# Batch 1's keys and queries through the DMA crossbar, in a kernel that joins chunked attention and a feed-forward layer

## The chip, the cores and the metric

The kernel runs on one core of one Trainium2 chip. The metric is the device time of that core in microseconds (us), from several executions. Those of the kernel before lay within 0.4% of their median. Each run has a mean granted TensorE clock (1.0 is full speed). A run counts as slow when it is over 1.5% above the fastest run of its kernel, and as fast otherwise, so that a "fast" run can have a clock below 1.0.

## The reference, cut to what matters

There are 4 batches of 8 heads, 768 tokens and 64 elements a head. Each chunk of 32 queries sees 16 keys to its left, 8 to its right, and 8 memory keys. The attention's output is normalised, and a feed-forward layer (512 to 2048 to 512) is added to it.

```python
for c in range(nc):                                  # nc = 768 / 32 chunks
    q_c = q[:, :, c_start:c_end]
    k_full = concat([mem_k, k[:, :, l_start:r_end]]) # up to 56 + 8 keys
    v_full = concat([mem_v, v[:, :, l_start:r_end]])
    a = softmax(scale * q_c @ k_full.T)
    out[:, :, c_start:c_end] = a @ v_full
# ... [cut: heads side by side give x, 768 x 512 a batch]
xn = (x - mu) / sqrt(var + 1e-06) * g_ln
return x + relu(xn @ w_ch1) @ w_ch2
```

The inputs are small (0.1 times normal numbers), so the softmax is nearly flat.

## The kernel before

The work is cut into 8 units of three tiles of 128 tokens; two units make a batch. Unit u runs its feed-forward matmuls (16 steps of "up", 12 of "down") and carries between its steps the attention of unit u+1 and the preparation of later batches. The function `at(step, ...)` puts a piece of work behind a step; each engine then executes its pieces strictly in that order. TensorE is the engine that is to be kept full.

Keys and queries have to stand with the 64 elements on the partitions before they can be multiplied. Batches 0 and 1 are loaded by rows and turned by TensorE; VectorE and ScalarE copy the result out of PSUM:

```python
    def turn_kq(pv, src, j, n):

        for r in range(8):
            for par in range(2):
                nc.tensor.matmul(
                    out=pv[64 * par : 64 * par + 64, n * r : n * r + n],
                    lhsT=src[0:n, 2 * j + par, r, :],
                    rhs=identity[0:n, 0:n],
                    is_transpose=True, start=True, stop=True,
                    tile_position=(0, 64 * par),
                )
# ...
    def kq_block(b, j, g0, g1, kind):

        pk, pq = slot("att"), None
        if kind == "att":
            pq = slot("att")
            pq = [pq[:, i, :] for i in range(2)]
        else:
            pq = [slot("mm")[:, :] for i in range(2)]
        for i in range(2):
            turn_kq(as16(pk[:, i, :]), k16[b % 2], j + i, 96)
        for i in range(2):
            turn_kq(as16(pq[i]), q16[b % 2], j + i, 96)
# ... [cut: keep_k on VectorE into KT, keep_q on ScalarE into QZ]
```

Batches 2 and 3 are loaded token by partition by GpSimd, turned by a DMA transpose (the "crossbar") issued from the sync queue, and finished by GpSimd, which copies neighbouring keys (`k_around`) and spreads the queries (`spread_q`):

```python
    def load_tokens(b, which, t):
        dst, src = ((kraw[0], k), (qraw[0], q))[which]
        nc.gpsimd.dma_start(
            out=free(dst, 512 * t, [[64, H], [1, 64]]),
            in_=dram(src, b * H * HS + 128 * t * D, [[D, 128], [HS, H], [1, 64]]),
        )

    def cross_k(b, half, t0, t1):
        nc.sync.dma_start_transpose(
            out=free(KT[b % 2], (24 * half + 4 * t0) * KR + 16, [[KR, 4 * (t1 - t0)], [1, 64]]),
            in_=kraw[0][64 * half : 64 * half + 64, 512 * t0 : 512 * t1],
        )

    def cross_q(half, t0, t1):
        nc.sync.dma_start_transpose(
            out=free(QT, (24 * half + 4 * t0) * 64, [[64, 4 * (t1 - t0)], [1, 64]]),
            in_=qraw[0][64 * half : 64 * half + 64, 512 * t0 : 512 * t1],
        )
# ...
    def spread_q(b, half, t0, t1):

        for par in range(2):
            rows = slice(64 * par, 64 * par + 64)
            nc.gpsimd.tensor_copy(
                out=QZ[b % 2][rows, 6 * half + t0 : 6 * half + t1, :, par, :],
                in_=QT[rows, (24 * half + 4 * t0) * 64 : (24 * half + 4 * t1) * 64].rearrange(
                    "p (t j x) -> p t j x", j=4, x=64),
            )
```

Batch 1's values come in 12 group loads, batches 2 and 3's in 8 head loads followed by copies of the edges (`v_around`) on the sync queue, where the outputs (in `down`) and from unit 3 on the transposes of x (`turn_x` with "dma") go too:

```python
    def v_around(b):

        vt = V[b % 2]
        nc.sync.dma_start(out=vt[0:16, 1:NG, :, :], in_=vt[64:80, 0 : NG - 1, :, :])
        nc.sync.dma_start(out=vt[80:88, 0 : NG - 1, :, :], in_=vt[16:24, 1:NG, :, :])
# ...
            nc.sync.dma_start(out=out[t // 6, 128 * (t % 6) : 128 * (t % 6) + 128, :], in_=o)
```

The plan of units 0 to 3, where the change lies:

```python
        if u == 0:
            at(1, clear_q, 1, 0)
            at(5, clear_q, 1, 1)
            at(14, clear_k, 1)
            at(16, clear_v, 1)
            for j in (0, 2):
                at(10 + j, kq_block, 0, j, 6, NG, "att")
                at(11 + j, keep_rest)
            for h in (0, 4):
                for which in range(2):
                    at(12, load_kq, 1, which, 0, 96, h, h + 4)
            for g in range(6):
                at(16, load_v_group, 1, g)
            attend(((16, 19, 19, 22), (17, 21, 21, 24), (19, 23, 23, 26)), "att")
            at(26, mem_cols, 1)
            at(26, v_mem, 1)
        elif u == 1:
            for j in (0, 2):
                at(5 + 3 * j, kq_block, 1, j, 0, NG, "att")
                at(7 + 3 * j, keep_rest)
            for g in range(6, NG):
                at(0, load_v_group, 1, g)
            for t in range(6):
                for which in range(2):
                    at(14, load_tokens, 2, which, t)
            attend(((16, 19, 19, 22), (17, 19, 20, 23), (21, 23, 23, 26)), "att")
        elif following:
            if u in (2, 4):
                attend(((2, 7, 7, 7), (4, 7, 8, 8), (9, 13, 13, 13)))
            else:
                attend(((9, 14, 14, 14), (11, 14, 15, 15), (16, 20, 20, 20)))
            if u == 2:
                cross((0, 0, 1, 1), 2, 0, 4, 3)
                at(8, mem_cols, 2)
                at(8, k_around, 2, 0, 4)
                for h in range(H):
                    at(8, load_v_head, 2, h)
                spread(9, 2, 0, 3)
                cross((14, 14, 15, 15), 2, 4, 6, 6)
            elif u == 3:
                at(1, v_mem, 2)
                at(1, v_around, 2)
                at(4, k_around, 2, 4, 6)
                spread(5, 2, 3, 6)
# ...
        for step in range(16 + 4 * n):
            if step < 16:
                up(u, n, step)
            else:
                i, part = divmod(step - 16, 4)
# ...
            for fn, args in plan.get(step, ()):
                fn(*args)
```

The softmax here doesn't subtract the row's maximum and nothing guards it: scores larger than these inputs give would overflow.

## Time and profile before

| | kernel before |
|---|---|
| median of the first 3 runs | 220.41 us (220.31 to 220.75) |
| median of the 4 runs beside the changed kernel | 220.52 us |
| span of the profiled run | 218.5 us |
| TensorE busy, granted clock | 97%, full |
| waits of TensorE over 0.25 us after unit 0 has begun | none |
| length of units 0 to 6 (first up matmul to the next unit's) | 27.80, 27.28, 23.38, 23.33, 23.35, 23.33, 23.33 us |

In the page, a digit of section 2 is one fortieth of the span, in tenths; the chain (section 4) shares out the span among the engines that held up the end. Units 0 and 1 are longer because their TensorE also turns keys, queries and x.

A transfer "lands" when its semaphore has been raised in full. The landing times of single transfers in this text are read from those updates in the trace; the views print only their medians.

Two timelines of the kernel before matter later. In timelines, columns are start, duration, engine, line, operation, tiles, count; what is in square brackets is the idle time before it and what ended it. First the DMA issues of GpSimd:

```profile
52.80 5.34 POOL L116 DMA_DIRECT2D V<-in_v_dram  x6
58.10 0.96 POOL L241 DMA_DIRECT2D kraw<-in_k_dram  x1
```

and those of the sync queue:

```profile
79.35 2.74 SPq L247 DMA_TRANSPOSE KT<-kraw  x2
82.26 2.61 SPq L253 DMA_TRANSPOSE kraw<-qraw  x2
86.48 6.42 SPq L345 DMA_TRANSPOSE xT<-xn  x3
...
103.51 0.60 SPq L130 DMA_DIRECT2D V<-V  x1
```

Batch 2's token loads start at 58.10. They have all landed by 72.2, so its first key transposes (79.35) find the DMA engines almost idle: issue takes 1.34 and 1.28 us, and the later one lands at 84.25, 3.4 us after its issue began. The edges of batch 2's values (103.51) are the last of that batch's work on the queue.

### The profile page before, as it was taken

The numbers are of one execution on the slowest core, as the hardware profiler recorded it, in microseconds if no ns is written. First come the engines' busy times: TensorE is split into PE (matmuls) and PEld (weight loads), VectorE is DVE, ScalarE is ACT, GpSimd is POOL, SyncE is SP. The second block draws the span as 40 slices with busy tenths as digits, with TensorE's granted clock in tenths as the row PEclk, the third lists the DMA queues.
The fourth block names the chain that finished last, engine by engine and source line by source line (L and its number), as shares of the span: only waits on it lengthen the run. The fifth ranks groups of instructions, "written<-read, shape, count | busy, mean of one in ns | idle before, by whom it ended". The sixth has DMA issues, their size and how long they took to land.

```text
span 218.5 us, 4954 instructions
## 1 busy us (share of the span) xinstructions
PE 212.8 (97%) x1975; PEld 129.2 (59%) x1975; DVE 118.7 (54%) x269; ACT 98.6 (45%) x196; POOL 105.0 (48%) x177
## 2 busy tenths in 40 slices
PE   7998999999999999999999999999999999999994
PEld 2554677556775577545764577446754676457553
DVE  6948566576764836823366339515386337534222
ACT  4464747635884766600555077202751165403200
POOL 7984435957995226986002999626174000300000
PEclk9999999999999999999999999999999999999999
DMA  4999999999999329995605799996743200330012
GB/s 74 181 146 206 208 202 170 192 204 193 178 145 150 105 91 128 163 139 178 87 2 99 106 176 156 162 183 96 174 122 99 96 0 11 88 103 21 0 48 96
DMA packets 93089, 27.20 MB, mean 124 GB/s; under 512 B 83673, under 2 KB 89561, under 8 KB 93018
## 3 DMA queue, kind: packets, MB, share of 16 engines
q0 software_dynamic: 67504, 14.23, 73.9%
q1 hardware_dynamic: 25562, 12.66, 24.7%
q8 instruction: 15, 0.25, 0.5%
q14 instruction: 8, 0.07, 0.1%
HBM read 28.48 MB, written 6.29 MB: 159 GB/s over the span
## 4 chain that ended last, share of the span: by engine, by line
PE 90%; DVE 3%; DMA 3%; ACT 1%; issue 1%; POOL 1%; DVEq 0%; POOLq 0%
PE mm L374 38%; PE mm L391 37%; PE att L288 5%; PE att L308 3%; DMA kraw<-in_k_dram 3%; PE att L178 2%; PE mm L409 2%; DVE xs L319 1%; ACT QZ L203 1%; DVE xn L328 1%; PE att L351 1%; PE mm L178 1%; PE att L365 1%; DVE QZ L203 1%; PE mm L365 0%
## 5 line engine op out<-in xcount | busy, mean ns | idle before, releaser
L374 PE MATMUL mm<-xT,w1c 128*128 128x384 f16 x512 | 88.5, 327 | 0.0
L391 PE MATMUL mm<-w2c,rT 128*128 128x512 f16 x368 | 84.2, 379 | 0.0
L374 PEld LDWEIGHTS <-w1c 128*128 128x128 f16 x512 | 56.8, 114 | 24.3 <-issue 0.3
L380 ACT ACTIVATE rT<-mm 128x384 f16<-128x384 f32 x64 | 31.2, 489 | 68.4 <-PE mm L374 46.8
L391 PEld LDWEIGHTS <-rT 128*128 128x128 f16 x368 | 34.8, 98 | 37.8
L382 DVE TENSOR_SCALAR rT<-mm 128x384 f16<-128x384 f32 x64 | 35.1, 554 | 35.9 <-PE mm L374 35.8
L398 DVE SCALAR_TENSOR_TENSOR osb<-mm,rstd,xs 128x512 f32<-128x512 f32 x23 | 17.3, 751 | 42.3 <-PE mm L391 29.9
L295 ACT ACTIVATE AT<-att,band 96x512 f16<-96x512 f32 x48 | 30.1, 678 | 10.9 <-PE att L288 10.6
L337 POOL TENSOR_SCALAR veps<-squares 128x1 f32<-128x1 f32 x24 | 4.6, 191 | 50.5 <-ACT junk L334 49.2
L116 POOL DMA_DIRECT2D V<-in_v_dram x24 | 21.5, 903 | 8.5 <-DMA w1c<-in_moe_w_ch_dram 4.3
L334 ACT ACTIVATE junk<-xs,nmean 128x512 f16<-128x512 f32 x24 | 17.3, 719 | 7.1 <-DVE nmean L325 6.7
L328 DVE SCALAR_TENSOR_TENSOR xn<-xs,nmean,g_row 128x512 f16<-128x512 f32 x24 | 18.5, 771 | 0.9
L319 DVE SCALAR_TENSOR_TENSOR xs<-att,rec 128x512 f32<-128x512 f32 x24 | 16.6, 692 | 0.8
L276 POOL COPY QZ<-kraw 64x768 f16<-64x768 f16 x16 | 14.4, 900 | 3.5 <-DMA kraw<-qraw 2.9
L203 ACT COPY QZ<-att 64x384 f16<-64x384 f16 (+1 forms) x20 | 12.0, 599 | 8.4 <-PE att L178 8.2
L288 PE MATMUL att<-QZ,KT 128*128 128x128 f16 x192 | 14.8, 219 | 0.2 <-DVE QZ L203 0.2
L288 PEld LDWEIGHTS <-KT 128*128 128x128 f16 x192 | 12.6, 98 | 4.0 <-issue 0.3
L341 POOL TENSOR_TENSOR rstd<-veps,mhalf 128x1 f32<-128x1 f32 x24 | 13.3, 552 | 2.0
L365 PE MATMUL mm<-busy 128*128 128x512 f16 x34 | 11.1, 454 | 1.2 <-DVE counts L455 1.2
L122 POOL DMA_DIRECT2D V<-in_v_dram x16 | 12.0, 807 | 0.0
L268 POOL COPY KT<-KT 128x128 f16<-128x128 f16 (+4 forms) x16 | 4.2, 293 | 15.6 <-DMA KT<-kraw 15.6
L241 POOL DMA_DIRECT2D kraw<-in_k_dram x12 | 11.4, 954 | 0.0
(68 smaller groups left out, 133.9 us busy)
## 6 DMA issues: line engine op xcount, KB each, us to landing
out_dram<-osb SPq DMA_DIRECT2D x23, 256.0 KB, 3.0
w1c<-in_moe_w_ch_dram POOLq DMA_DIRECT2D x4, 512.0 KB, 10.0
w2c<-in_moe_w_ch_dram POOLq DMA_DIRECT2D x4, 512.0 KB, 14.2
V<-in_v_dram POOLq DMA_DIRECT2D x20, 88.0 KB, 8.5
kraw<-in_k_dram POOLq DMA_DIRECT2D x12, 128.0 KB, 4.5
qraw<-in_q_dram POOLq DMA_DIRECT2D x12, 128.0 KB, 4.6
V<-in_v_dram POOLq DMA_DIRECT2D x16, 96.0 KB, 5.3
kraw<-in_k_dram POOLq DMA_DIRECT2D x3, 256.0 KB, 6.2
```

What stands on the lines that cost most here:

```text
L116: nc.gpsimd.dma_start(out=V[b % 2][r : r + hi - lo, g, :, 0:64], in_=dram(v, b * H * HS + lo * D, [[64, hi - lo], [HS, H], [1, 64]]),)
L203: copy(out=free(QZ[b % 2][rows, g0, j, par, :], 0, [[512, g1 - g0], [8, 8], [1, 8]]), in_=free(pv[rows, :], 8 * g0, [[8, g1 - g0], [1, 8], ...
L288: nc.tensor.matmul(out=p[:, gg, 128 * j : 128 * j + 128], lhsT=KT[b % 2][:, (4 * g + j) * KR : (4 * g + j) * KR + 128], rhs=QZ[b % 2][:, g ...
L295: nc.scalar.activation(out=free(a, 32 * c, [[512, 2], [64, 8], [1, 32]], KR), in_=free(p, 32 * c, [[512, 2], [64, 8], [1, 32]], KR), func= ...
L319: nc.vector.scalar_tensor_tensor(out=x.rearrange("p (h d) -> p h d", h=H), in0=free(p, 0, [[128, H], [1, 64]]), scalar=1.0, in1=free(r, 0, ...
L328: nc.vector.scalar_tensor_tensor(out=xn[i], in0=x, scalar=nmean[i], in1=g_row, op0=ALU.add, op1=ALU.mult,)
L334: nc.scalar.activation(out=junk, in_=xs[xi], func=ACTF.Square, bias=nmean[i], accum_out=squares[i],)
L374: nc.tensor.matmul(out=p, lhsT=free(w, i, [[4, 128]]), rhs=xT[u % 2][:, dt, 0 : 128 * n], start=(dt == 0), stop=(dt == 3),)
L380: nc.scalar.activation(out=o, in_=p, func=ACTF.Relu)
L382: nc.vector.tensor_scalar(out=o, in0=p, scalar1=0.0, scalar2=None, op0=ALU.max)
L391: nc.tensor.matmul(out=p, lhsT=rT[hc][:, 128 * i : 128 * i + 128], rhs=w2c[hc // 4][:, hc % 4, :], start=(hc == 0), stop=(hc == 15),)
L398: nc.vector.scalar_tensor_tensor(out=o, in0=p, scalar=rstd[t % 9], in1=xs[t % 9], op0=ALU.mult, op1=ALU.add,)
```

## The change

Batch 1 is to go the way of batches 2 and 3. TensorE loses 128 transposes; in exchange twelve token loads (128 KB each) take the place of four larger ones, eight crossbar transposes join the sync queue, all twelve value loads move behind the first crossbar part, the first half of the queries is spread by VectorE and ScalarE, and the attention of unit 2 stands one step later. A "crossbar part" below is a group of four transposes, two of keys and two of queries: batch 1's first part serves the scores of unit 2's tiles (computed during unit 1), its second part those of unit 3's.

```diff
-    QT = kraw[1]
+    QT = sb.tile([128, NG * 4 * 64], FP16, name="QT")
# ... [cut: sizes of kraw and qraw, k16 and q16 for batch 0 alone, place() for b > 0]
-        dst, src = ((kraw[0], k), (qraw[0], q))[which]
+        dst, src = ((kraw[b % 2], k), (qraw[b % 2], q))[which]
# ... [cut: the same in cross_k and cross_q]
-    def spread_q(b, half, t0, t1):
+    def spread_q(b, half, t0, t1, copy=nc.gpsimd.tensor_copy):
# ...
         if u == 0:
-            for h in (0, 4):
+            for t in range(6):
                 for which in range(2):
-                    at(12, load_kq, 1, which, 0, 96, h, h + 4)
-            for g in range(6):
-                at(16, load_v_group, 1, g)
+                    at(12, load_tokens, 1, which, t)
# ...
         elif u == 1:
-            for j in (0, 2):
-                at(5 + 3 * j, kq_block, 1, j, 0, NG, "att")
-                at(7 + 3 * j, keep_rest)
-            for g in range(6, NG):
-                at(0, load_v_group, 1, g)
+            cross((0, 0, 1, 1), 1, 0, 4, 3)
+            at(2, k_around, 1, 0, 4)
+            for g in range(NG):
+                at(2, load_v_group, 1, g)
+            at(14, spread_q, 1, 0, 0, 3, nc.vector.tensor_copy)
+            at(14, spread_q, 1, 1, 0, 3, nc.scalar.copy)
+            cross((15, 15, 16, 16), 1, 4, 6, 6)
+            at(18, k_around, 1, 4, 6)
+            spread(18, 1, 3, 6)
             for t in range(6):
                 for which in range(2):
-                    at(14, load_tokens, 2, which, t)
-            attend(((16, 19, 19, 22), (17, 19, 20, 23), (21, 23, 23, 26)), "att")
+                    at(19, load_tokens, 2, which, t)
+            attend(((17, 20, 20, 23), (18, 20, 21, 24), (21, 24, 24, 27)), "att")
```

More of the change, by code (lines that the diff above doesn't have):

```diff
@@ L57 @@
     w2c = [sb.tile([128, 4, 512], FP16, name=f"w2c{i}") for i in range(4)]
-    kraw = [sb.tile([128, 4096], FP16, name=f"kraw{i}") for i in range(2)]
-    qraw = [sb.tile([128, 4096], FP16, name=f"qraw{i}") for i in range(2)]
-    QT = kraw[1]
-    k16 = [t[0:96, 0:4096].rearrange("p (h r d) -> p h r d", h=H, r=8) for t in kraw]
-    q16 = [t[0:96, 0:4096].rearrange("p (h r d) -> p h r d", h=H, r=8) for t in qraw]
+    kraw = [sb.tile([128, 3072 if i else 4096], FP16, name=f"kraw{i}") for i in range(2)]
+    qraw = [sb.tile([128, 3072 if i else 4096], FP16, name=f"qraw{i}") for i in range(2)]
+    QT = sb.tile([128, NG * 4 * 64], FP16, name="QT")
+    k16 = kraw[0][0:96, :].rearrange("p (h r d) -> p h r d", h=H, r=8)
+    q16 = qraw[0][0:96, :].rearrange("p (h r d) -> p h r d", h=H, r=8)
     V = [sb.tile([128, NG, H, HD], FP16, name=f"V{i}") for i in range(2)]
@@ L106, in load_kq @@
         nc.gpsimd.dma_start(
-            out=dst[b % 2][lo:hi, h0:h1, :, :],
+            out=dst[lo:hi, h0:h1, :, :],
             in_=dram(src, (b * H + h0) * HS + 512 * lo,
@@ L216, in kq_block @@
         for i in range(2):
-            turn_kq(as16(pk[:, i, :]), k16[b % 2], j + i, 96)
+            turn_kq(as16(pk[:, i, :]), k16, j + i, 96)
         for i in range(2):
-            turn_kq(as16(pq[i]), q16[b % 2], j + i, 96)
+            turn_kq(as16(pq[i]), q16, j + i, 96)
         def keep(i):
@@ L236, in place @@
     def place(b, g):
-        return g if b < 2 else g % 2 * (NG // 2) + g // 2
+        return g if b == 0 else g % 2 * (NG // 2) + g // 2
     def load_tokens(b, which, t):
-        dst, src = ((kraw[0], k), (qraw[0], q))[which]
+        dst, src = ((kraw[b % 2], k), (qraw[b % 2], q))[which]
         nc.gpsimd.dma_start(
@@ L248, in cross_k, with cross_q @@
             out=free(KT[b % 2], (24 * half + 4 * t0) * KR + 16, [[KR, 4 * (t1 - t0)], [1, 64]]),
-            in_=kraw[0][64 * half : 64 * half + 64, 512 * t0 : 512 * t1],
+            in_=kraw[b % 2][64 * half : 64 * half + 64, 512 * t0 : 512 * t1],
         )
-    def cross_q(half, t0, t1):
+    def cross_q(b, half, t0, t1):
         nc.sync.dma_start_transpose(
             out=free(QT, (24 * half + 4 * t0) * 64, [[64, 4 * (t1 - t0)], [1, 64]]),
-            in_=qraw[0][64 * half : 64 * half + 64, 512 * t0 : 512 * t1],
+            in_=qraw[b % 2][64 * half : 64 * half + 64, 512 * t0 : 512 * t1],
         )
@@ L270, in k_around @@
             )
-    def spread_q(b, half, t0, t1):
+    def spread_q(b, half, t0, t1, copy=nc.gpsimd.tensor_copy):
         for par in range(2):
             rows = slice(64 * par, 64 * par + 64)
-            nc.gpsimd.tensor_copy(
+            copy(
                 out=QZ[b % 2][rows, 6 * half + t0 : 6 * half + t1, :, par, :],
@@ L511 @@
     for j in range(2):
-        turn_kq(first_k[j], k16[0], j, CUT)
+        turn_kq(first_k[j], k16, j, CUT)
     for j in range(2):
-        turn_kq(first_q[j], q16[0], j, CUT)
+        turn_kq(first_q[j], q16, j, CUT)
     for j in range(2):
@@ L522 @@
     for j in range(2, 4):
-        turn_kq(first_k[j], k16[0], j, CUT)
+        turn_kq(first_k[j], k16, j, CUT)
     stay_busy(5, spare)
     for j in range(2, 4):
-        turn_kq(first_q[j], q16[0], j, CUT)
+        turn_kq(first_q[j], q16, j, CUT)
     for j in range(2, 4):
@@ L583, in cross @@
                 at(steps[half], cross_k, b, half, t0, t1)
-                at(steps[2 + half], cross_q, half, t2 - 3, t2)
+                at(steps[2 + half], cross_q, b, half, t2 - 3, t2)
         def spread(step, b, t0, t1):
```

## The prediction

> **What bounds the kernel now.** I read the page first (busy shares, then the chain that ended last), then the chain in order of time, then the groups of instructions by shape, and last the timelines of ScalarE, GpSimd and the sync queue around the stretch that changes.
>
> ```profile
> PE 212.8 (97%) x1975; PEld 129.2 (59%) x1975; DVE 118.7 (54%) x269; ACT 98.6 (45%) x196; POOL 105.0 (48%) x177
> PEclk9999999999999999999999999999999999999999
> DMA  4999999999999329995605799996743200330012
> PE 90%; DVE 3%; DMA 3%; ACT 1%; issue 1%; POOL 1%; DVEq 0%; POOLq 0%
> ```
>
> The reader sees TensorE busy 97% at full granted clock, and 90% of the chain on it. Outside the first 22 us there is almost no gap, so a TensorE instruction taken out there shortens the run by its time, unless what replaces it makes TensorE wait. The DMA row is 9 from about 5 to 71 us: the stretch in which batch 1 is loaded has little DMA time to spare. The chain in time order shows what is taken out:
>
> ```profile
> 50.56 3.90 PE mm L374 x24
> 54.46 1.48 PE att L178 x64
> 55.94 4.02 PE mm L374 x24
> 59.97 1.48 PE att L178 x64
> 61.45 2.73 PE mm L374 x16
> ...
> 76.76 0.22 PE att L351 x4
> 76.98 0.86 PE mm L391 x4
> 77.84 1.95 PE mm L374 x12
> ```
>
> L178 is the transpose of keys and queries on TensorE. The two pieces of 64 are batch 1's, 1.48 us each, both on the chain, with no wait around them. The last three lines are the end of unit 1 (a unit is three tiles of 128 tokens; unit 1 runs from 50.56 to 77.84): the last transpose of x, four matmuls of the down projection, then unit 2's up projection.
>
> **What the Trainium skill says.** (1) "TensorE: Matmul & The Clock Gate", Part 4: a TensorE transpose costs some 275 ns in a kernel's context. The trace disagrees about the cost in a stream: single records last 206 ns, but they overlap, and 64 take 1.48 us, 23 ns each. I use 1.48. (2) "DMA: Bandwidth & Descriptors", Specifications: below 512 B a transfer is not at line rate. Agrees: batch 2's token loads (head rows of 64 elements, 256 B read and 128 B written, 1024 pieces in 128 KB) land 0.85 us apart when queued, 154 GB/s of fp16; batch 1's old loads (rows of 512 elements, 384 pieces in 384 KB) land 1.9 us apart, 207 GB/s. So the same 1.5 MB takes 10.3 us in place of 7.6. (3) The same page, DMA Transpose (X-bar): 2-byte types, issued from sync or scalar queues only; so the eight new transposes join the one sync queue that also carries outputs and the later transposes of x. Batches 2 and 3 already do this in the trace. (4) The same page, "Anatomy of one DMA": DMA engines don't wait on semaphores, the issuing queue does. So a transpose that waits for its load holds everything behind it on the sync queue; the trace shows the queue issuing strictly in order.
>
> **The change, part by part.**
>
> *Removed.* 128 transposes of batch 1: 2 x 1.48 = 2.96 us on the chain. Also 12 VectorE copies into KT (5.4 us) and 8 ScalarE copies into QZ (6.3 us); neither engine held TensorE there, so they count nothing.
>
> *Loads, batch 1.* GpSimd issues them from 38.7 us as before (the roots ahead of them are the same). Earlier transfers drain until 43.0 (the landing of the last one). Old: four loads, landed at 44.8, 46.7, 48.7, 50.6. New: twelve at 0.85 to 0.87 us each, issue cost 0.95: landed by 43.0 + 12 x 0.87 = 53.4; the seventh, with which all keys of the first part are in, at 49.1.
>
> *First crossbar part.* The sync queue is free of outputs at 52.1 (before: last output issue 51.51, 0.55 long). Four transposes at about 1.3 us issue: 52.1 to 57.3. To landing, from batches 2 and 3:
>
> ```profile
> KT<-kraw SPq DMA_TRANSPOSE x8, 4.2
> kraw<-qraw SPq DMA_TRANSPOSE x8, 3.1
> kraw<-in_k_dram POOLq DMA_DIRECT2D x12, 128.0 KB, 4.5
> ```
>
> They stand behind three outputs that took 5 to 6.7 us to land in this congested stretch, so I put keys at 57 to 58.5 and queries at 59 to 60.5.
>
> *Values.* Their 12 loads now follow the neighbours' copies (0.4 + 0.79 us in batch 2) that wait for the keys. GpSimd starts them at about 59, 0.9 us apart, done at 70; landing 4.5 us after issue: groups 0 to 3 at 63.5, 64.4, 65.3, 66.3. Needed: unit 1 without transposes reaches step 16 at 50.56 + 16 x 0.65 = 60.96; steps 16 to 20 at 0.86 each plus two scores at 0.45 give 66.2 for the first values. Tile 0 is met; tile 1 (groups 2, 3) is just met. I charge 0.4 us.
>
> *Query spread on VectorE and ScalarE, step 14.* Behind TensorE's 60.3 to 60.9; ScalarE's two copies take about 1.6 us (the old ones of that size 1.60), so until 62.3, scores want it at 62.7. Met, charge 0.1.
>
> *Last transpose of x a step later (27, not 26).* In the trace before, ScalarE's copy ran under the four down matmuls:
>
> ```profile
> 77.02 0.59 ACT L356 COPY xT<-att 128x512 f16<-128x512 f16 x1 [1.10 <-PE att L351]
> ```
>
> It ends at 77.61, 0.63 after the transposes' end at 76.98, and 0.86 of matmuls covered it. Now nothing follows in unit 1, and unit 2's first matmul needs the copy: an exposed wait of 0.65 to 0.7 us. This is the one certain cost.
>
> *Batch 2, pushed back.* GpSimd: values until 70, second neighbours' copies 0.9, four spreads 3.5 (done 74.5; scores want them at about 77.5), then twelve token loads from 74.5 instead of 58.1. The seventh lands at about 84, so the crossbar of batch 2 starts at 84 instead of 79.35; four issues end at 89.3, and unit 3's three transposes of x, behind them on the same queue, issue 89.3 to 92.7 instead of 86.48 to 92.9. Before, they took up to 5.9 us to land beside value loads: the last at 97 to 98.5. Unit 3 starts at 101.2 - 2.2 = 99.0. Slack 0.5 to 2: charge 0.2 on average. Later stages have more room: batch 2's scores at 105.5, its queries spread by about 100.5.
>
> Sum: -2.96 + 0.67 + 0.4 + 0.1 + 0.2 = -1.6; 220.41 - 1.6 = 218.8. Since the waits may well be nil, I take **218.7 us**.
>
> **Rivals.**
> *A, clean gain:* all new work is hidden and even the 0.67 is partly covered: 217.5 to 218.1. For it: batches 2 and 3 already go this way without a wait on TensorE. Against: they have their loads a unit ahead; batch 1 has 10 us.
> *B, late values take the place of the transposes:* if the keys' crossbar lands after 60 (congestion with outputs and the token loads' tail), values land at 66 to 69 and TensorE waits 1 to 3 us at step 20: 219.5 to 221.5. For it: value loads in this stretch took 4.5 to 10 us to land. Against: in the new kernel GpSimd's queue is empty by 53.4, so the transposes have the engines almost alone.
> *C, sync queue becomes the bound at unit 3:* token loads of batch 2 hold the queue and x of unit 3 comes late, 1 to 3 us: 219.5 to 221. For: 16 us of delay on GpSimd. Against: batch 2's slack absorbs most.
> *D, GpSimd as a chain* (copies, 12 value loads, copies, spreads, 12 token loads, back to back from 58 to 86): spreads after 77.5 would hold unit 2's scores. Slack 3 us; it would come only together with B.
>
> **Range and chances.** Best case is the full 2.96 less part of 0.67: 217.4. B or C in their middle give 220 to 221; both together more. Range 217.4 to 220.8. Faster by over 2% needs 216.0, more than the chain offers: 2%. Slower by over 2% needs 224.9, over 7 us of new waits: 4%. Within 2%: 94%. In sign I expect a gain of about 0.8%.
>
> **What would show it.** Right: no L178 after 35 us; unit 1 about 2 to 3 us shorter; a gap of 0.6 to 0.7 on TensorE ahead of unit 2's first up matmul, ended by the ScalarE copy L356; KT transposes issued at 52 us; value loads at 58 to 70; gap at L308 near 66 under 1 us. Wrong: a gap over 1 us at the first L308 or L288 of batch 1 ended by a DMA or a copy (B), or at the first L374 of unit 3, about 99 us, ended by the transposes of x (C), or VectorE or ScalarE held by the spread long enough to stop the up matmuls.

## The result

| | before | after |
|---|---|---|
| median of 4 runs | 220.52 us | 223.83 us |
| range | 220.31 to 220.75 | 222.41 to 225.83 |
| profiled run: time, span, clock | 220.25, 218.5, 0.998 | 223.66, 222.0, 1.0 |
| length of unit 1 | 27.28 | 28.30 |
| length of unit 2 | 23.38 | 24.90 |
| length of unit 3 | 23.33 | 24.68 |
| units 0, and 4 to 6 | 27.80; 23.35, 23.33, 23.33 | the same |

Three of the four runs after are fast, at full clock; 225.83 is slow (clock 0.992). The ratio is 1.0129 (95%: 1.0079 to 1.0178). A ratio here is the mean time of one kernel's fast runs over that of the other's fast runs of the same rounds, so not quite the ratio of the medians. The change loses some 1.3%. I had expected a gain of 0.8%, and the range I gave ended at 220.8.

The page of the changed kernel, the lines that answer to those of before (busy shares, the DMA row of the slices, the chain by engine):

```profile
PE 210.2 (95%) x1847; PEld 126.7 (57%) x1847; DVE 115.3 (52%) x259; ACT 94.3 (42%) x190; POOL 118.2 (53%) x197
DMA  5999999999899999999923599997643300321012
PE 73%; DMA 14%; DVE 4%; POOL 2%; issue 2%; SPq 2%; ACT 1%; POOLq 0%; DVEq 0%
```

TensorE does have 128 instructions and 2.6 us less to do, yet its share falls and DMA's share of the chain goes from 3% to 14%. In the DMA row of before, the 14th and 15th slices (71 to 82 us) were 3 and 2: engines only 20 to 40% busy. After, the row is 8 or 9 from the second slice to the twentieth, up to 111 us. The timeline of TensorE shows the new waits (all over 0.25 us after unit 0 has begun):

```profile
63.99 0.38 PE L288 MATMUL att<-QZ,KT 128*128 128x128 f16 x4 [1.54 <-ACT QZ L276]
...
69.37 0.41 PE L308 MATMUL att<-V,AT 96*64 96x65 f16 x15 [1.19 <-DMA V<-in_v_dram]
...
78.20 2.11 PE L374 MATMUL mm<-xT,w1c 128*128 128x384 f16 x12 [0.67 <-ACT xT L356]
...
103.10 6.69 PE L374 MATMUL mm<-xT,w1c 128*128 128x384 f16 x40 [1.39 <-DMA xT<-xn]
...
115.19 0.70 PE L308 MATMUL att<-V,AT 96*64 96x65 f16 x32 [1.25 <-DMA V<-V]
```

The first three lie in unit 1: the late queries of batch 1, its late values (0.20 us more of the same kind at 67.99), and the copy of x that nothing covers now. The fourth stands before unit 3, the fifth inside it. Together 6.24 us; less the 2.96 us of transposes, that is 3.3 us: 0.6 in unit 1 (waits of 3.60) and 2.64 in unit 3. The two profiled runs differ by 3.4 us, but the close agreement is partly luck. From the first up matmul of unit 0 to that of unit 4 the run after takes 105.68 us and the run before 101.79, so 3.89 more; the run after had begun unit 0 0.5 us earlier. The 0.6 us beyond the idle times is some 0.1 us at each restart (unit 3 is 1.35 us longer for a wait of 1.25 inside it). From unit 4 on both take 94.2 us, so nothing is left to look for there. GpSimd shows how work is pushed back:

```profile
58.43 0.40 POOL L268 COPY KT<-KT 128x256 f16<-128x256 f16 x1 [5.92 <-DMA KT<-kraw]
...
60.59 10.68 POOL L116 DMA_DIRECT2D V<-in_v_dram  x12
...
72.49 3.44 POOL L276 COPY QZ<-QT 64x768 f16<-64x768 f16 x4
75.88 0.91 POOL L241 DMA_DIRECT2D kraw<-in_k_dram  x1
```

It stands idle for 5.92 us waiting for batch 1's keys, then issues twelve value loads, spreads queries, and only at 75.88 starts batch 2's token loads, 17.8 us later than before. The sync queue follows:

```profile
51.68 5.86 SPq L247 DMA_TRANSPOSE KT<-kraw  x2
...
86.48 4.84 SPq L247 DMA_TRANSPOSE KT<-kraw  x2
91.49 2.60 SPq L253 DMA_TRANSPOSE QT<-qraw  x2
94.19 3.84 SPq L345 DMA_TRANSPOSE xT<-xn  x3
...
107.62 1.80 SPq L130 DMA_DIRECT2D V<-V  x1
```

Batch 2's first key transposes wait for the seventh token load (landed at 86.4), so unit 3's x goes out at 94.19 rather than 86.48, and the edges of the values at 107.62 rather than 103.51. Note also 51.68: two key transposes took 5.86 us to issue here, where batch 2's two took 2.74 us in the kernel before at 79.35.

The edges have a second constraint, which nearly coincides with the queue's. They copy batch 2's values, whose last load landed at 106.67 here and at 95.04 before, since GpSimd issued those loads behind its wait for batch 2's keys (94.42 for 85.03). Freeing the queue alone could have let the edges go at most 0.95 us earlier.

### The profile page after: what moved, and what is told of

Read it like the earlier page. It is cut to its first block, busy times and chain, and to the rows that moved or that the text cites.

```text
span 222.0 us, 4717 instructions
## 1 busy us (share of the span) xinstructions
PE 210.2 (95%) x1847; PEld 126.7 (57%) x1847; DVE 115.3 (52%) x259; ACT 94.3 (42%) x190; POOL 118.2 (53%) x197
## 4 chain that ended last, share of the span: by engine, by line
PE 73%; DMA 14%; DVE 4%; POOL 2%; issue 2%; SPq 2%; ACT 1%; POOLq 0%; DVEq 0%
PE mm L391 30%; PE mm L374 28%; DMA KT<-kraw 6%; PE att L288 4%; PE att L308 3%; DMA xT<-xn 3%; PE mm L365 3%; DMA V<-in_v_dram 3%; DMA V<-V 3%; PE mm L409 2%; PE att L178 1%; POOL V L116 1%; POOL KT L268 1%; DVE xs L319 1%; PE att L365 1%
## 5 line engine op out<-in xcount | busy, mean ns | idle before, releaser
L116 POOL DMA_DIRECT2D V<-in_v_dram x24 | 21.4, 899 | 7.3 <-DMA w1c<-in_moe_w_ch_dram 4.5
L337 POOL TENSOR_SCALAR veps<-squares 128x1 f32<-128x1 f32 x24 | 5.3, 220 | 35.9 <-ACT junk L334 34.4
L276 POOL COPY QZ<-QT 64x768 f16<-64x768 f16 x20 | 16.9, 843 | 3.0 <-DMA QT<-qraw 2.3
L268 POOL COPY KT<-KT 128x128 f16<-128x128 f16 (+4 forms) x24 | 6.7, 308 | 21.3 <-DMA KT<-kraw 21.2
L319 DVE SCALAR_TENSOR_TENSOR xs<-att,rec 128x512 f32<-128x512 f32 x24 | 16.6, 691 | 0.8
L241 POOL DMA_DIRECT2D qraw<-in_q_dram x18 | 16.9, 938 | 0.0
L241 POOL DMA_DIRECT2D kraw<-in_k_dram x18 | 16.9, 938 | 0.0
L308 PEld LDWEIGHTS <-AT 96*64 96x64 f16 x384 | 7.8, 111 | 9.2 <-issue 5.8
L308 PE MATMUL att<-V,AT 96*64 96x65 f16 x384 | 9.8, 197 | 3.0 <-DMA V<-in_v_dram 1.4
```

What stands on the lines that cost most here:

```text
L116: nc.gpsimd.dma_start(out=V[b % 2][r : r + hi - lo, g, :, 0:64], in_=dram(v, b * H * HS + lo * D, [[64, hi - lo], [HS, H], [1, 64]]),)
L241: nc.gpsimd.dma_start(out=free(dst, 512 * t, [[64, H], [1, 64]]), in_=dram(src, b * H * HS + 128 * t * D, [[D, 128], [HS, H], [1, 64]]),)
L308: nc.tensor.matmul(out=p[64 * gg : 64 * gg + 64, h // 4, c0 : c0 + 65], lhsT=AT[t % 3][0:KR, gg, h, :], rhs=V[b % 2][0:KR, 2 * t + gg, h, ...
L319: nc.vector.scalar_tensor_tensor(out=x.rearrange("p (h d) -> p h d", h=H), in0=free(p, 0, [[128, H], [1, 64]]), scalar=1.0, in1=free(r, 0, ...
```

## The experiments

Having seen this I held two theories. The **order theory**: the in-order queues of GpSimd and sync pass a delay of batch 1 on to batch 2, and this costs unit 3. The **room theory**: from about 38 to 92 us the DMA engines have no time to spare, so that whatever is moved ahead there puts something else back. The rivals were that single placements are to blame (the outputs ahead of the crossbar, the order of values and keys), which would be mended by moving one thing. Of the experiments all results but e10's agreed with the reference. Two kernels (e6, e10) work on wrong data.

### Is the removed work worth what I said? (e5)

The kernel before, with batch 1's transposes done twice:

```diff
+        if b == 1:
+            for i in range(2):
+                turn_kq(as16(pk[:, i, :]), k16[b % 2], j + i, 96)
+            for i in range(2):
+                turn_kq(as16(pq[i]), q16[b % 2], j + i, 96)
```

Expected:

> The kernel BEFORE with batch 1's 128 transposes of keys and queries done twice on TensorE (the second writes the same values over the first; result correct). Theory (the term removed is 2.96 us of TensorE time on the path, read as 2 pieces of 1.48): 2.9 to 3.2 us longer, 222.9 to 223.4 us against 220.0. Rival (part of these transposes runs in the shadow of something else, and the term was over-sized): under 2.5 us longer.

Measured: median 223.15 us (222.68 to 223.53) against 220.18, ratio 1.0130 (1.0106 to 1.0153): 2.9 us for 128 more transposes. So the first term of my sum, 2.96 us, is right, and the loss must lie in what was added.

### Only the delay of batch 2 (e3)

The kernel before, with nothing of the change in it, except that batch 2's token loads are issued late:

```diff
-                    at(14, load_tokens, 2, which, t)
+                    at(26, load_tokens, 2, which, t)
```

Expected:

> The kernel BEFORE, nothing of the change in it, but with batch 2's token loads held behind unit 1's first root on GpSimd, so that they start at about 76 us (as in the changed kernel, 75.9) and not at 58. Theory (the waits of unit 3 come from these loads being late alone, by way of the sync queue): the crossbar transposes of batch 2 start at 86 to 87 us, and TensorE waits 1 to 1.7 us for x of unit 3 at about 101 to 103 us and 1 to 1.7 us for the values around at about 115 us: 222.5 to 224 us. Rival (the waits of unit 3 need batch 1's second crossbar part, the single query tile or the new value loads): no such waits, within 0.5 us of the kernel before.

Measured: median 223.84 us (222.49 to 226.55) against 219.96; ratio 1.0153 (1.0097 to 1.0209). The verdict by the 2% rule is unclear, but the loss is plain. TensorE's timeline has two waits and no other over 0.25 us; GpSimd's first token load stands beneath them:

```profile
101.49 6.69 PE L374 MATMUL mm<-xT,w1c 128*128 128x384 f16 x40 [0.70 <-DMA xT<-xn]
...
114.89 0.70 PE L308 MATMUL att<-V,AT 96*64 96x65 f16 x32 [2.56 <-DMA V<-V]
```

```profile
75.51 0.96 POOL L241 DMA_DIRECT2D kraw<-in_k_dram  x1
```

The loads start at 75.51, as in the changed kernel (75.88), and the same two instructions wait: 3.26 us in sum, where the changed kernel has 2.64. The delay of batch 2 by itself costs about 3.4 us, as much as the whole loss. This is the order theory's cleanest evidence.

### Unit 3 set free in two ways (e6, e7)

First, the changed kernel without batch 2's token loads: batch 2's transposes read batch 1's tokens. The data are wrong. (The comparison with the reference did pass it, which tells only how little the nearly flat softmax shows of wrong keys.)

```diff
-            in_=kraw[b % 2][64 * half : 64 * half + 64, 512 * t0 : 512 * t1],
+            in_=kraw[1 if b == 2 else b % 2][64 * half : 64 * half + 64, 512 * t0 : 512 * t1],
# ... [cut: the same for qraw]
-            for t in range(6):
-                for which in range(2):
-                    at(19, load_tokens, 2, which, t)
```

> WRONG RESULT ON PURPOSE: the changed kernel without batch 2's twelve token loads; its crossbar transposes read batch 1's keys and queries, which lie ready (so batch 2's output is wrong). Theory (unit 3's waits come from batch 2's loads being late, by way of the sync queue): crossbar of batch 2 starts at 78.5 us for 86.5, no wait of TensorE at x of unit 3 nor at the values around (2.6 us less), the waits of unit 1 and of unit 2's head stay (3.4 to 4.5 us): 220.5 to 221.5 us. Rival (unit 3 waits for another reason, for instance the eight value loads of batch 2 being late): waits at unit 3 stay, 223 us or more.

Measured: median 221.65 us (220.91 to 223.51), ratio 1.0081 (1.0034 to 1.0129). The total missed the expected 220.5 to 221.5 narrowly; the profiled run (220.91) lies inside it. Batch 2's key transposes are issued at 78.45, unit 3 is back to 23.33 us without a wait, and what is left are the waits of unit 1 (0.62, 1.89 and 0.68 us: 3.19, against 2.96 saved) and one of 0.27 us in unit 2.

Second, the changed kernel with correct data, and with batch 2's work ordered so that unit 3's x and the edges of the values no longer stand behind the late transposes:

```diff
             if u == 2:
-                cross((0, 0, 1, 1), 2, 0, 4, 3)
-                at(8, mem_cols, 2)
-                at(8, k_around, 2, 0, 4)
                 for h in range(H):
-                    at(8, load_v_head, 2, h)
-                spread(9, 2, 0, 3)
-                cross((14, 14, 15, 15), 2, 4, 6, 6)
+                    at(5, load_v_head, 2, h)
+                at(8, mem_cols, 2)
+                cross((14, 14, 15, 15), 2, 0, 4, 3)
+                at(17, k_around, 2, 0, 4)
+                spread(18, 2, 0, 3)
# ... [cut: in unit 3 the second part behind v_around, its copies at step 10]
```

> The changed kernel with late loads of batch 2 left as they are, but the sync queue reordered: unit 3's transposes of x ahead of batch 2's crossbar, the second crossbar part behind the values around, batch 2's value loads ahead of the wait for keys on GpSimd. Theory (the late loads cost time only because the sync queue is in order and what they hold up stands behind them): x of unit 3 issues at 86 to 93 us as in the kernel before, values around land before 110, no waits in unit 3: 220.5 to 221.5 us. Rival (the lateness itself, or the DMA engines' load, sets it): keys of batch 2 late for their scores at 108 us, or x still late by contention: 222.5 us or more.

Measured: median 222.35 us (221.24 to 224.15), ratio 1.0108 (1.0049 to 1.0168); expected were 220.5 to 221.5. The sync queue in the profiled run (221.45 us):

```profile
87.47 6.60 SPq L345 DMA_TRANSPOSE xT<-xn  x3
94.26 3.72 SPq L247 DMA_TRANSPOSE KT<-kraw  x2
98.14 3.02 SPq L253 DMA_TRANSPOSE QT<-qraw  x2
...
104.70 0.59 SPq L130 DMA_DIRECT2D V<-V  x1
```

The x of unit 3 now leads, the edges go out at 104.70, and no wait is left in units 2 and 3 (23.57 and 23.33 us). Both experiments confirm the order theory for this part. (e7 also issues batch 2's value loads earlier on GpSimd, the last one landing at 100.77 for 106.67, so it doesn't tell the sync queue's share of the edges' delay from that of the loads.) The waits of unit 1 remain (1.20, 0.86, 1.29 and 0.67 us), and they alone eat more than the 2.96 us. Of the correct versions with all of batch 1 on the crossbar it has the lowest median, though its interval overlaps that of the change itself (1.0079 to 1.0178), and it doesn't beat the kernel before.

### Unit 1, one placement at a time (e1, e2, e11, e4)

**e1**: the third tile a step earlier, so that four matmuls cover the copy of x again.

```diff
-            attend(((17, 20, 20, 23), (18, 20, 21, 24), (21, 24, 24, 27)), "att")
+            attend(((17, 20, 20, 23), (18, 20, 21, 24), (21, 23, 23, 26)), "att")
```

> The changed kernel with the last tile of unit 1 (values, norm, transpose of x) one step earlier, as in the kernel before (23, 23, 26). Theory (an exposed copy of 0.67 us at the head of unit 2, a cost of its own): that gap goes, unit 2 starts 0.7 us earlier than in the changed kernel (77.5 for 78.2 us). But since the transposes of x of unit 3 are set by the sync queue and not by TensorE, the waits at 103 and 115 us grow by as much: total gain 0 to 0.7 us. Rival (all waits add up independently): the full 0.7 us is gained.

Measured: 224.05 us (222.83 to 225.55), ratio 1.0186 (1.0130 to 1.0242); against 1.0129 for the change itself, in other rounds. The gap of 0.67 us is gone, as it should be, but no gain shows in the totals. TensorE's timeline of e1:

```profile
63.95 0.38 PE L288 MATMUL att<-QZ,KT 128*128 128x128 f16 x4 [0.88 <-ACT QZ L276]
...
70.06 0.41 PE L308 MATMUL att<-V,AT 96*64 96x65 f16 x15 [2.07 <-DMA V<-in_v_dram]
...
102.39 6.69 PE L374 MATMUL mm<-xT,w1c 128*128 128x384 f16 x40 [0.82 <-DMA xT<-xn]
...
114.80 0.70 PE L308 MATMUL att<-V,AT 96*64 96x65 f16 x32 [1.58 <-DMA V<-V]
```

The values are waited for longer (2.07 for 1.39), the queries less (0.88 for 1.54). The expectation that the waits of unit 3 would grow by as much as the copy's went did not come true: they are 2.40 us in sum, where the change has 2.64. In the profiled runs units 0 to 3 even take 104.64 us rather than 105.68, but the runs of either kernel spread by some 3 us. So e1 leaves open what the copy alone costs.

**e2**: the first crossbar part issued from unit 0, ahead of that unit's outputs. I wanted to know why the first keys took until 58.4 to land: because the outputs were ahead of them on the queue ("O"), or because the tail of the token loads was still in flight ("L").

```diff
+            cross((23, 23, 24, 24), 1, 0, 4, 3)
             at(26, mem_cols, 1)
# ...
         elif u == 1:
-            cross((0, 0, 1, 1), 1, 0, 4, 3)
```

> The changed kernel with the first crossbar part of batch 1 (four transposes) ahead of unit 0's three outputs on the sync queue, so that nothing stands before it but its own loads (the seventh landed at 49.2 us). Theory O (the outputs ahead on the queue made it late): transposes issue at 49.2 us, the first keys land by 53.5, the second by 55; waits of TensorE at batch 1's scores and values (1.5 + 1.4 us) gone, and GpSimd 3 us ahead afterwards, so that unit 3's waits shrink from 2.6 to under 0.5 us: 217.5 to 219 us. Theory L (the token loads still in flight slow it, until 52.6 us): keys land at 55.5 to 57 whatever is ahead, waits at batch 1 halved, unit 3's too: 219.5 to 221.5 us.

Measured: 228.75 us (225.74 to 231.27), ratio 1.0351 (1.0276 to 1.0425). The first keys, issued at 48.58 with no output ahead, landed at 55.76, still 7.2 us later: the tail alone is enough (L). The scores no longer wait. But the second part now met outputs and value loads: its two key transposes took from 58.47 to 65.22 to issue and landed at 70.25 and 71.67. TensorE's timeline of e2 has three waits for values and one far away (and, not shown, 0.67 us for the copy and 1.83 us for unit 3's x):

```profile
66.91 0.41 PE L308 MATMUL att<-V,AT 96*64 96x65 f16 x15 [0.99 <-DMA V<-in_v_dram]
68.47 0.19 PE L308 MATMUL att<-V,AT 96*64 96x65 f16 x1 [1.15 <-DMA V<-in_v_dram]
69.41 0.60 PE L308 MATMUL att<-V,AT 96*64 96x65 f16 x15 [0.75 <-DMA V<-in_v_dram]
...
118.75 0.70 PE L308 MATMUL att<-V,AT 96*64 96x65 f16 x32 [2.93 <-DMA V<-V]
```

The granted clock was halved for 3.41 us twice, from 69.07 (in the first group) and from 120.27 (after the last wait). The landing was foreseen, the total was not, by either theory.

**e11** (one look): only the seven token loads that the first part needs stay ahead; the other five follow six of the values.

```diff
-            for t in range(6):
-                for which in range(2):
+            for t in range(4):
+                for which in range(2 if t < 3 else 1):
                     at(12, load_tokens, 1, which, t)
# ... [cut: the other five before the seventh value load]
```

> The changed kernel with only the seven token loads that the first crossbar part reads ahead of it; the other five issue behind the first six value loads. One look, for the landing of the first part; the second part will be late and the total no better. Theory L (token loads still in flight slow the first part): nothing is in flight but outputs, and the keys, issued at 51.7 us, land by 55.5 and 57. Theory O (the three outputs ahead on the sync queue slow it): keys land at 57.5 to 60 as in the changed kernel (58.4 and 59.8).

Measured: 234.87 us in its one run (state unknown; clock 0.971). The token loads in flight were over at 48.8, and still the first keys, issued at 52.28 behind three outputs (landed at 51.7, 54.7 and 56.7) and one small copy of memory values, landed at 57.84. So here the outputs are enough (O), and the tail isn't needed. With e2: either company makes 5.6 to 7.2 us out of a landing that took 3.4 us in the kernel before at 80.8. The total is much worse because the second half of batch 1's queries now came 5.06 us late in unit 2.

**e4**: six of the value loads right behind the token loads, as in the kernel before.

```diff
+            for g in range(6):
+                at(16, load_v_group, 1, g)
# ...
-            for g in range(NG):
+            for g in range(6, NG):
                 at(2, load_v_group, 1, g)
```

> The changed kernel with batch 1's first six value loads back right behind the token loads (not behind the first crossbar part); the other six stay behind it. Theory (the values wait because GpSimd waits for the keys' crossbar before it issues them): the waits at batch 1's values (0.2 + 1.2 us) go, and GpSimd reaches batch 2's token loads some 5 us earlier (70.5 for 75.9), so unit 3's waits (1.4 + 1.3 us) go too; the wait for the queries' spread (1.5 us) stays or grows a little: 218.5 to 220.5 us. Rival (contention): the value loads in flight slow the crossbar part by 2 us or more, keys land after 60 us, the spread's wait grows to 3 us or more: 221 us or more.

Measured: 227.24 us (226.14 to 227.84), ratio 1.0322 (1.0283 to 1.0361). No wait on values is left, and none in unit 3, but the keys landed at about 64.6. TensorE's timeline of e4:

```profile
66.81 0.38 PE L288 MATMUL att<-QZ,KT 128*128 128x128 f16 x4 [4.24 <-DVE QZ L276]
68.57 0.59 PE L288 MATMUL att<-QZ,KT 128*128 128x128 f16 x4 [1.38 <-ACT QZ L276]
```

The six value loads and the keys changed places in the same stretch of DMA time: what the expectation's rival, and the room theory, had said. The granted clock was also halved for 6.83 us (67.69 to 74.51): unit 1 took 33.69 us, some 3.1 more than its waits explain (27.28 - 2.96 + 4.24 + 1.38 + 0.67 = 30.61).

### Everything that I had learnt at once (e8), and without the values (e10)

e8 takes e7's order, spreads both halves of the queries on VectorE, moves unit 2's scores a step later, and holds the second crossbar part back until unit 1's first output is out.

```diff
-            at(14, spread_q, 1, 1, 0, 3, nc.scalar.copy)
-            cross((15, 15, 16, 16), 1, 4, 6, 6)
+            at(14, spread_q, 1, 1, 0, 3, nc.vector.tensor_copy)
+            cross((19, 19, 20, 20), 1, 4, 6, 6)
# ...
-            attend(((17, 20, 20, 23), (18, 20, 21, 24), (21, 24, 24, 27)), "att")
+            attend(((18, 21, 21, 24), (19, 21, 22, 25), (22, 24, 24, 27)), "att")
# ... [cut: k_around and spread at 21, token loads at 23, unit 2 three steps later, e7's order]
```

> The reordered kernel of the run before, and in unit 1: both halves of the queries' spread on VectorE, batch 1's scores one step later, second crossbar part behind the first output of unit 1, so that the first value loads have the DMA engines to themselves; attention of unit 2 three steps later. Theory (unit 1's waits are late queries, 1.5 us, and value loads slowed by the second crossbar part, 1.4 us): waits in unit 1 fall from 3.4 to about 1.2 us (0.67 of it the copy at unit 2's head), total 218 to 219.3 us, faster than both. Rival (the DMA engines have more work in 40 to 90 us than they can do, so that a wait moved shows up elsewhere): 220.5 us or more.

Measured: 227.72 us (225.35 to 230.21), ratio 1.0309 (1.0249 to 1.0368). The rival came true. Unit 1 is what the two certain terms of the prediction give: 24.99 us = 27.28 - 2.96 + 0.67. But the second part, issued at 66.1, landed at 80.6, 14.4 us later, beside the last six value loads, which were held up as well (they landed from 74.1 to 80.6). Unit 2 pays, as TensorE's timeline of e8 shows:

```profile
80.68 0.38 PE L288 MATMUL att<-QZ,KT 128*128 128x128 f16 x4 [1.29 <-POOL QZ L276]
82.43 0.52 PE L288 MATMUL att<-QZ,KT 128*128 128x128 f16 x4 [1.36 <-POOL QZ L276]
```

Units 2 and 3 took 28.45 and 27.62 us, and the clock was halved twice for 3.41 us. The wait was moved on, not removed.

e10 is e8 without batch 1's value loads; the values are read from the other buffer, so the result is wrong (relative error 0.586).

> WRONG RESULT ON PURPOSE: e8_both (227.7 us) without batch 1's twelve value loads; batch 1 reads batch 0's values. In e8_both the second crossbar part issued at 66 us and its last queries landed at 80.6. Theory (it lay in flight with the value loads, and together they were more than the DMA engines do in that time): without the loads the part lands within 5 to 7 us of its first issue (by 73), no wait in units 2 and 3, 217.8 to 219 us, and the half clock that followed the waits is gone. Rival (its place behind the output, or on the sync queue, makes it late): it lands after 76 and unit 2 still waits: 221 us or more.

Measured: 234.89 us (234.53 to 235.40), ratio 1.0674. The second part, issued at 65.7, landed at 73.6: 7.9 us where e8 took 14.4, and just outside the 5 to 7 that I had expected. So the value loads were what it shared the engines with, and the room theory holds for the landing. The total I had expected missed by far, through a flaw of the experiment: the buffer that I let unit 2 read is the one that batch 2's value loads fill, and TensorE waited for those. Its timeline:

```profile
92.24 0.27 PE L308 MATMUL att<-V,AT 96*64 96x65 f16 x2 [9.14 <-DMA V<-in_v_dram]
```

So e10 says nothing of the time that a free DMA stretch would give.

### How much room is there? (e9, e12)

**e9**: only batch 1's queries go by the crossbar; the keys stay on TensorE, with the loads that they had. That is half of the saving (1.48 us) for half of the new transfers.

```diff
+            for t in range(3):
+                at(12, load_tokens, 1, 1, t)
+            for h in (0, 4):
+                at(12, load_kq, 1, 0, 0, 96, h, h + 4)
# ... [cut: the other three query loads, six values, cross_q from step 23 of unit 0 and step 1 of unit 1]
```

> Half of the change: of batch 1 only the queries go token by partition and by crossbar (first part issued at about 46 us, ahead of unit 0's outputs; their spread on ScalarE and VectorE); the keys stay on TensorE as in the kernel before, so that GpSimd waits for no crossbar, and value loads and batch 2's token loads keep their old places. Theory (half the gain, 1.48 us, is there; what cost time was GpSimd's wait for the keys, which put batch 2's loads off, and the load on the DMA engines, here half): batch 2's loads start at 58 to 60 us, no wait of TensorE over 0.5 us: 218.5 to 219.3 us against 220.1, ratio 0.992 to 0.997. Rival (the DMA engines have no room in this stretch for even half): crossbar of the second part or batch 2's loads late, waits of 1 us or more in unit 1 or 3: 220 us or more.

Measured over 5 rounds: median 221.68 us (219.69 to 227.78), ratio of the fast runs 1.0042 (1.0003 to 1.0081). The two slow runs (224.87 and 227.78) had clocks of 0.985 and 0.977. The profiled run (220.08 us) has waits of 0.33 and 0.71 us only. The last value load landed at 71.9 (61.9 before), and batch 2's token loads began at 65.93 (58.10 before), although GpSimd waits for no crossbar here: it waits for landings of earlier loads (3.72 us before 61.65). The rival came true in the late loads and the total, not in waits of 1 us or more. In the profiled runs units 0 to 3 take 101.60 us for 101.79: the two waits and the restarts after them ate nearly all of the 1.48 us.

**e12**: the kernel before, plus twelve transposes of 128 KB into tiles that nobody reads, from unit 1's start on. TensorE and GpSimd have the same work as before; only the DMA engines and the sync queue have more.

```diff
+            for t0 in (0, 2, 4):
+                for i in range(4):
+                    at(t0, idle_cross, (kraw[1], qraw[1])[i // 2], i, t0 + i % 2)
```

> The kernel BEFORE, with as much crossbar traffic as the change adds (1.5 MB, twelve transposes of 128 KB from batch 1's loaded keys and queries, issued from 52 us on behind unit 0's outputs) into tiles that nobody reads, so that no engine waits for them and the order on GpSimd stays; result correct. Theory D (the DMA engines have no room in this stretch): batch 1's last value loads land at 66 to 72 us for 61.9, batch 2's last token load at 78 to 83 for 72.2, waits of TensorE at batch 1's values or in unit 3 of 1.5 us or more, 221.7 us or more. Theory G (GpSimd's in-order wait for the keys is what cost the time, the engines had room): value loads and token loads less than 4 us later than before, 220.0 to 220.7 us.

Measured: four runs, 220.26 and 220.94 us (fast, full clock), 223.82 and 227.51 us (slow, clocks 0.990 and 0.985); the kernel before beside it 220.29. The last value load of batch 1 landed at 68.5 rather than 61.9, and batch 2's last token load at 92.1 rather than 72.2: the landings are put back as the room theory (D in the text) has it. Yet in the profiled run (220.94) one wait over 0.3 us came of it in TensorE's timeline:

```profile
112.73 0.70 PE L314 MATMUL att<-V,AT 96*64 96x65 f16 x32 [0.98 <-DMA V<-V]
```

The kernel before has slack enough to take nearly all of this in the fast runs; of their totals one is what theory G had expected (220.0 to 220.7) and one is 0.24 us above. The seventh of batch 2's token loads, for which the sync queue waits, landed at 79.9, where the change has it at 86.4. The edges were issued at 106.14, right behind the last value load (landed at 105.94), though the queue had been free since 103.09: here it was the loads that held them. I read this so: transfers alone mostly use up slack, and the loss comes when an order of work also needs the landing. The two slow runs, which were not traced, may tell otherwise.

## Why the prediction was wrong

**Right.** The removed work (2.96 us; e5 gave 2.9). The certain cost of 0.67 us for the uncovered copy of x, met to the digit at 78.20. Token loads landed by 52.6, the last at 55.65 (53.4 predicted); the first crossbar issue at 51.68 (52.1); the value loads' issue from 60.59 to 71.3 (59 to 70). No instruction of L178 is left after unit 0.

**The terms that were mis-sized.** "I charge 0.4 us" for the values: measured 1.39. I had them land 0.9 us apart from 63.5 on, the pace of their issue; they landed at 64.46, 66.45, 67.95 and 69.33, 1.4 to 2 us apart, beside the second crossbar part, which was issued in just that time (60.45 to 66.20) and which that step left out. (In e8, which moves that part to 66.14, the first four landed 1.2 to 1.4 us apart and nothing waited for them; they were also wanted a step later.) "Met, charge 0.1" for the spread of the queries: measured 1.54. I took 1.3 us for each issue; the first took 4.46, so that ScalarE's half could start only at 62.3 and ended at 63.9. "Charge 0.2 on average" for batch 2's delay: measured 1.39 before unit 3, since unit 3's x was issued from 94.19 and not from 89.3: the seventh token load landed 2.4 us later than I had put it, and the key transposes took 4.84 us to issue where I had counted 2.6.

**The step that failed outright.** "Later stages have more room: batch 2's scores at 105.5". I looked at the scores, and not at the last thing on the same queue: the edges of batch 2's values, issued at 107.62 and needed at 113.9. 1.25 us, in no term of mine. The loads that the edges copy from were late as well (106.67), by way of GpSimd. e3 shows this wait (2.56 us) with nothing of the change in the kernel, e6 and e7 show it go when batch 2's delay, or its order, is taken away. In all the waits came to 6.24 us where my sum had 1.37: 1.44 more for the queries, 0.99 for the values, 1.19 for x and 1.25 for the edges.

**The rivals.** B and C were both on paper with waits of 1 to 3 us, and waits of both kinds came together (1.39 us each). C's mechanism is the right one. B's is right in part: its condition, keys that land after 60, was not met (the neighbours' copies began at 58.43 and 59.86), and the values were late all the same. "Both together more" stands in the prediction, but the range ended at 220.8 and left that case out. The two have a common root: both the value loads and batch 2's token loads stand on GpSimd behind its wait for batch 1's keys (5.92 us). Against B I had written that "the transposes have the engines almost alone". They had three outputs and the last token loads beside them, and e2 and e11 show that either of these is enough.

Two small slips of its sums bear on nothing: 217.4, the low end, is 220.41 less the full 2.96 with no part of the 0.67 added, and 2% above 220.41 is 224.8.

**Shown, and not shown.** That batch 2's delay makes the loss of unit 3 is shown (e3, e6, e7). That landings in this stretch depend on what else is in flight is shown (e2, e8 with e10, e11, e12), as the Trainium skill has it in "DMA: Bandwidth & Descriptors", "Issuing engines are not separate DMA queues": transfers of sync, scalar and gpsimd run on the same 16 engines and interleave. That this makes a gain impossible is only argued: seven ways of moving the work gave none, but e10, which was to free the stretch, was spoilt. How the engines share out their time between loads and transposes, and why some runs of the more crowded kernels are 3 to 8 us longer at a lower clock (e9, e12), stays open. A hint: one halving of 3.41 us in a span of 222 us makes a mean clock of 0.992, two make 0.985 and three 0.977, which are about the clocks of the slow runs (0.992 after the change, 0.985 and 0.977 in e9, 0.990 and 0.985 in e12). They may be runs in which waits grew long enough to halve the clock, and then fast runs alone understate the loss. No slow run was traced, so this is not shown.

## What to carry to other kernels

Before work is moved from a full engine to the DMA queues, list every later item on each in-order queue behind it, down to the last one, and put a time to each, and to the loads that it needs; the item that pays may be two stages away. Take landing and issue times from a stretch as busy as the one that the work goes to: the 3.4 us of one transpose in a quiet stretch were 5.6 to 7.2 us here. And when a wait that ends with a transfer is taken away and nothing is gained, look for the transfer that changed places with it.

## What the Trainium skill lacked or had wrong

- "TensorE: Matmul & The Clock Gate", Why this matters for your kernels, asks for no idle gaps over some 3 us between bursts, lest the clock falls. In these runs the length of one gap does not decide: the clock was halved after 1.29 and 1.36 us with 0.4 us of matmuls between them (e8, from 82.54 us), not after a single 2.56 us (e3). What the page has of the window, 3413 ns and free-running (What's actually happening), agrees: the shortest halvings lasted 3.41 us, others two steps (6.83 in e4) or five (17.07 in e10), and all changes of one trace lie a whole number of 3.41 us steps apart. Counted in these steps, a full clock was halved behind every step with 1.90 us or more of idle TensorE (1.90 and 2.55 in e2, 2.65 and 2.30 in e8, 3.03 in e4) and behind none with 1.80 or less; the 2.56 us of e3 fell into two steps, 1.63 and 0.93.
- The same page, Part 4, has some 275 ns for one 128x128 transpose in a kernel's context, and no figure for a stream of them; here 64 (of 96x64) took 1.48 us, and 128 more of them cost 2.9 us (e5), 23 ns each.
- "DMA: Bandwidth & Descriptors", DMA Transpose (X-bar), has no figure for a transpose beside other traffic. A key transpose landed 3.4 us after issue with the engines almost idle (batch 2's second, kernel before), 6.7 us beside outputs and token loads (batch 1's first, after), and a part of four transposes took 14.4 us beside value loads (e8) where it took 7.9 us without them (e10). Nor does it say that the issue itself is held up: 1.3 us in the quiet stretch, 4.46 us after, 4.70 us in e2.
- No page gave a way to foresee that GpSimd's loads are held at issue when many are in flight: batch 2's twelve token loads took 10.6 us to issue in the kernel before and 16.6 us in e12, with waits of up to 1.81 us between them.
